# Loading a matrix a second time in turned form, and turning only its solved half on the chip

## The chip, the cores and the metric

The kernel runs on one core of a Trainium2 chip. The metric is the device time of one execution in microseconds (us). A profile of one execution stands beside it: it lists every instruction of the engines TensorE (PE; its weight loads are PEld), VectorE (DVE), ScalarE (ACT), GpSimd (POOL) and SyncE (SP, which here only issues transfers), with the clock that TensorE was granted.

## The reference

Two stages follow one another. The first is a recurrence over 768 time steps, for 4 x 8 heads of width 40:

```
for t in range(S):
    y[:, :, t] = np.einsum('bhd,bhde->bhe', rt, state)
    Sa = np.einsum('bhde,bhe->bhd', state, at)
    state_decay = state * wt[:, :, None, :] - np.einsum('bhd,bhe->bhde', Sa, bt)
    state = state_decay + np.einsum('bhd,bhe->bhde', vt, kt)
```

The second takes the 3072 rows of y (320 wide) as tokens of a mixture of experts: each token goes to the best of 8 experts by x @ w_gate, up to a capacity, through relu(x @ w1) @ w2, scaled by its gate.

## The kernel before

The recurrence is done in chunks of 64 steps: 12 chunks (q), each for two halves of the batch (pr 0 and 1), so 24 units of 16 heads each. Two chunks make one iteration i (128 steps, 6 of them). Per iteration the rows w, a, k and b are loaded and decayed (`decay`, `decay_k`, on DVE), products of the chunk with itself are made (`nn`, `kk`, `iden`), and a triangular system is inverted (`inverse`, `join`, `comb`, mostly a chain on DVE). Per unit a chain then follows, which the state ties to the unit of the chunk before:

1. `zz` and `zz_s` multiply v and the state into a right hand side; `sa` applies the inverse; `take_sa` copies the 64 solved rows beside the 64 loaded rows of v in the tile `vu`. So half of the 128 partitions of `vu` holds v and the other half holds what was solved.
2. `uT` turns `vu` with eight TensorE transposes of 128x128; `take_uT` (ACT, in one unit DVE) copies the result from PSUM to the tile `vT`, 128x1024. There is one `vT`.
3. `mT` multiplies `vT` by `rv`; `take_m` masks it into `vu`; `yy` makes the output rows and the new state; `take_snew` and `take_y` take these.

The output is gated (`gate`, `logits`), routed (`route`: tables of rows for each expert), and stored to `xd`. The experts then gather rows from `xd`, turn them by a transfer, and multiply: `p00` and `p10` are the first parts of experts 0 and 1, whose tokens come from the first four iterations; `p01`, `p11`, `p2` to `p7` follow and need the whole table. Their weights are loaded, and split by ACT and DVE into two halves of 16 bits, in the buffers that the recurrence gives up (`hand_...`).

All engines run in the order of one list, `ORDER`, written out by hand as text. A name is one step, `*2` repeats it, `/1` takes the second choice of engines, and `~3` puts three idle multiplies (`warm`, L197: `ident` by `ident`, 128x512) ahead of it on TensorE. Each engine works through its own instructions in the order of the list and waits where an operand or buffer is not there. All loads and stores of the recurrence are issued by SP in that order too. They are spaced: `dma` lets a transfer start only when the third last one before it has landed (the fifth last for the first twenty).

Of the kernel before, what the change touches and what calls it, by code (L numbers as in the profile page):

```python
# [10 lines left out]
F32 = mybir.dt.float32  # L11
# [8 lines left out]
P = 128  # L20
# [20 lines left out]
out0 iden1 fill chain1 inverse join/1 out0 load_a join join_sw out0 decay0 join iden1 gate0 join decay0 load_rv
turn1 logie0 uT1 load_kb gate0 join load_kb load_v uT1 out1 gate0*2 join logie0 lower_w out1/1 join out1 zz0 decay0
chain0 lower comb out1 comb out1 iden0 decay_k0 chain0 turn0 comb~1 lower decay_k0 turn0/1 gate0 load_a unit comb
turn1~1 decay1 iden0 gate1*2 load_kb comb decay_k1 logie0 turn1 inverse_0 comb load_v gate1 decay1 zz1*2 logie1~3
comb chain0~2 chain0 chain1*2 decay1 logie1 nn0 uT0*2 load_kb nn0/1 nn1~1 logie1 nn1 nn0 out0 nn0 chain1 load_w
decay_k1 nn1~1 out0/1 chain1 uT1 decay0 load_rv nn1 inverse zz0~1 inverse*2 out0 uT1 inverse out0 out1 inverse*2
chain0 logie0 inverse*2 out0 load_w turn0~1 inverse*2 zz1 chain0 gate1 tk_ chain0~1 out1/1 inverse*2 load_v inverse
kk inverse*3 turn0 inverse gate1 chain0 kk out1 uT0 out1 load_a out1 zz1 chain1 iden1 turn1 uT0 inverse out0 chain1
inverse tk_ iden0~1 iden1 kk inverse out0 chain1 iden0 inverse kk out0~1 chain1/1 iden0 zz0 out0 load_a load_v
join_sw join out0 chain0 join chain0 join decay0 iden0 join gate0 load_kb*2 decay0 uT1 decay_k0 gate0 uT1 gate0  # L50
join*2 load_rv logie1 turn1 join lower_w out1 out1/1 comb iden1 load_kb logie0 load_v comb decay_k0 out1 logie0/1
comb iden1 gate0/1 turn0 decay1 out1 lower comb lower/1 nn0 inverse_0 out1 turn0 unit comb~3 zz1~3 nn0 decay1 comb
decay_k1 logie0 zz1 gate0 decay1 turn1 chain0~1 load_kb comb decay_k1 chain1 nn0 chain0 nn1 chain1 uT0 nn0/1 nn1
uT0/1 logie0 nn1 chain1 out0 chain1 nn1/1 out0/1 uT1 load_rv uT1 gate1~2 turn1 inverse out1 inverse*2 out0 out1/1
gate1 inverse load_v inverse gate1 inverse*2 out1 inverse*2 out0 zz0 chain0 load_v inverse logie1 inverse turn0
inverse out0 chain0 out1 inverse out1 inverse zz1 tk_ load_v logie1/1 inverse gate1/1 inverse chain0*2 inverse zz1
kk inverse*2 uT0 chain1 kk inverse uT0 gate1 iden0 turn0 iden0 chain1 logie1 load_w load_a iden1 tk_ out0 inverse
iden1 chain1 load_w chain1 out0/1 join_sw join kk load_a join out0 decay0 out0 kk/1 join*2 iden0~1 out0 iden0 turn1
decay0 join uT1 join load_kb zz0 turn1 gate0 logie1 uT1 out1~2 gate0 decay0 load_v load_kb lower_w logie0 join gate0
out1/1 comb gate0 chain0 logie0/1 chain0 comb out1 lower decay_k0*2 out1 zz1 logie0 out1 iden1*2 lower decay1 comb  # L60
gate1~5 turn0 logie0 load_rv gate0 comb zz1 decay1 gate1 decay1 comb load_kb gate1 chain1 logie1~1 comb*2 turn0/1
chain0*2 load_kb inverse_0 tk_ decay_k1 load_rv turn1 logie1 chain1/1 turn1/1 nn0 nn1 nn0 load_w chain1 decay_k1 kk
chain1 uT0 nn1/1 kk/1 nn0 nn1 unit uT0 out0 nn0 decay0 nn1 out0/1 inverse*2 uT1~1 out0 logie1 inverse out0 inverse*2
zz0 inverse*2 load_v chain0 uT1 inverse out0 inverse gate1/1 chain0 out1 inverse turn0 load_w out1/1 chain0 inverse
chain0 turn0 inverse*2 load_a out1 inverse*2 logie1 inverse out1*2 zz1*2 uT0*2 chain1*2 iden1 out0 load_a iden1
inverse*2 tk_ inverse kk out0 iden0 kk chain1 load_v iden0 out0 inverse*2 chain1/1 zz0 join out0 iden0 join chain0
gate1 out0 uT1~1 chain0 join_sw/1 decay0 join uT1 join load_rv decay0 out1 out1/1 load_kb gate0~1 iden0 turn1
decay_k0 gate0 turn1/1 gate0 join~1 join*2 load_v out1 comb/1 lower out1 nn0 out1 comb load_kb lower gate0 load_v
comb decay_k0 comb inverse_0 gate0 turn1 lower_w/1 iden1 nn0 comb gate1~2 logie1 iden1 decay1 comb*2 chain0~3
load_kb turn1/1 zz1 gate1 decay1 logie1 turn0 gate1 load_kb zz1 chain1 chain0 uT0 nn0~2 chain1 decay1 uT0 gate1  # L70
chain1 out0 decay_k1 chain1 nn1 turn0 nn0/1 out0/1 logie1 unit nn1 hand_z logie1 decay_k1 uT1 kk nn1~2 uT1 tk_ nn1
out0 inverse load_rv out1 hand_px out0 logie0 kk out0 iden1 logie0 out1/1 logie0 inverse zz0 chain0 inverse*2 iden1
# [272 lines left out]
def scan_part(tc, keep, one, psum, w, a, kb, rv, vt, w_gate, wge, xd, lg, ident, up, SX, route, fill):  # L345
# [116 lines left out]
    def prep(pr, i):  # L462
# [57 lines left out]
        def mul_a():  # L520
            engine().tensor_mul(T["a"][0:R], T["a"][0:R], T["px"][0:R, :, 0:P])  # L521
# [1314 lines left out]
```

## Time and profile before

| | |
|---|---|
| median of 3 runs | 569.18 us (567.82 to 573.0) |
| profiled execution | 565.18 us, of which the span from first to last instruction is 563.5 us |
| mean granted clock of TensorE | 0.986 |
| busy: PE, DVE, ACT, POOL | 515.7, 407.6, 304.5, 124.3 us |
| moved by DMA | 81.34 MB |

Busy time is the time in which an engine works at something that the profile counts. An engine can be less than fully busy and still set the pace, if others always wait for it; which one waits for which is read from the list of waits. TensorE's matrix multiplies overlap in the records, so that the time of a step on TensorE is read from the distance of starts.

### The profile page before, as it was taken

What the parts mean: (1) busy time and instruction counts of PE and PEld (TensorE: products, weight loads), DVE (VectorE), ACT (ScalarE), POOL (GpSimd) and SP (SyncE); (2) the same over time, 40 slices, a digit from 0 to 9 for tenths busy, and PEclk for the clock granted to TensorE, in tenths of its full rate; (3) what the DMA queues carried; (4) which work ended last, traced back from release to release, by engine and by line L of the source; (5) the groups of instructions that cost most, each with busy time, mean ns of one, the idle gap of its engine ahead of it and who ended that gap; (6) DMA issues with size and microseconds to landing.
All of it is one profiled execution on the core that took longest, in us unless ns stands there. A gap on an engine that the chain in (4) does not pass through costs nothing.

```text
span 563.5 us, 24790 instructions
## 1 busy us (share of the span) xinstructions
PE 515.7 (92%) x11145; PEld 383.5 (68%) x11145; DVE 407.6 (72%) x671; ACT 304.5 (54%) x572; POOL 124.3 (22%) x173
## 2 busy tenths in 40 slices
PE   0979899999989999999999997997999999999994
PEld 0545688778968887888888885665746465564652
DVE  8999899898979999989799876771536626444140
ACT  4344547867864688559654544542545435553230
POOL 9400010006001100020110023033265042730113
PEclk9999999999999999999999999898999999999998
DMA  8674055543613652445202328658789594992201
GB/s 267 196 208 123 4 137 173 178 125 121 189 57 101 177 179 59 119 154 151 71 24 76 137 88 219 182 159 230 177 255 229 150 265 151 227 196 88 57 24 53
DMA packets 77769, 81.34 MB, mean 144 GB/s; under 512 B 34684, under 2 KB 58366, under 8 KB 77652
## 3 DMA queue, kind: packets, MB, share of 16 engines
q1 hardware_dynamic: 74324, 70.21, 44.8%
q0 software_dynamic: 3328, 9.44, 5.5%
q8 instruction: 89, 1.46, 1.2%
q14 instruction: 28, 0.23, 0.1%
HBM read 63.90 MB, written 10.88 MB: 133 GB/s over the span
## 4 chain that ended last, share of the span: by engine, by line
PE 20%; issue 18%; DVE 6%; DMA 5%; POOL 5%; POOLq 0%; ACT 0%; SPq 0%; DVEq 0%
PE pp L404 8%; PE pp L1644 5%; POOL out_dram L1518 3%; PE p L1512 3%; DMA xT<-a 2%; DMA a<-xd,ri 2%; POOL a L1489 2%; DMA out_dram<-tk,ri 1%; PE pp L904 1%; PE pp L197 1%; DMA px<-in_moe_w_dram 1%; PE p L942 0%; PE pp L578 0%; DVE ns L1451 0%; PE pp L1036 0%
## 5 line engine op out<-in xcount | busy, mean ns | idle before, releaser
L454 POOL TENSOR_SCALAR_AFFINE_SELECT tk<-tk 64x512 f32<-64x512 f32 x28 | 20.6, 737 | 156.6 <-ACT tk L451 112.4
L1518 POOL DMA_INDIRECT out_dram<-tk,ri x26 | 34.1, 1311 | 94.1 <-ACT tk L1679 69.9
L197 PE MATMUL pp<-ident 128*128 128x512 f16 x145 | 40.8, 394 | 9.0 <-ACT pp L422 3.2
L404 PE MATMUL pp<-a,kb 64*64 64x64 f32 x1536 | 30.8, 224 | 11.9 <-DVE a L521 11.1
L404 PEld LDWEIGHTS pp<-a,kb 64*64 64x64 f32 x1536 | 26.3, 136 | 20.6 <-DVE a L521 13.6
L404 PE MATMUL pp<-vu,bk 128*40 128x104 f32 (+1 forms) x768 | 38.7, 252 | 1.7 <-issue 0.8
L1489 POOL DMA_INDIRECT a<-xd,ri x26 | 27.4, 1053 | 42.9 <-DVE gs L1408 26.4
L404 PEld LDWEIGHTS pp<-vu,bk 128*40 128x40 f32 x768 | 33.0, 117 | 4.6 <-issue 1.6
L1644 PE MATMUL pp<-xT,z 128*128 128x448 f16 (+2 forms) x128 | 30.7, 332 | 5.8 <-DMA xT<-a 5.8
L143 ACT COPY vT<-pp 128x1024 f32<-128x1024 f32 x23 | 23.3, 1013 | 21.7 <-PE pp L904 16.7
L1644 PE MATMUL pp<-xT,ns 128*128 128x448 f16 (+2 forms) x192 | 32.4, 307 | 0.4 <-DVE ns L1451 0.4
L586 ACT ACTIVATE bk<-pp,few 128x320 f32<-128x320 f32 x48 | 22.7, 527 | 16.1 <-PE pp L578 15.2
L143 ACT COPY zs<-pp 64x320 f32<-64x320 f32 x44 | 18.5, 420 | 23.2 <-PE pp L404 21.5
L526 DVE TENSOR_TENSOR kb<-kb,gx 104x1024 f32<-104x1024 f32 x24 | 28.9, 1216 | 2.1 <-DMA kb<-in_kb_dram 2.0
L508 DVE TENSOR_TENSOR_SCAN gx<-px,z 104x1032 f32<-104x1032 f32 (+1 forms) x13 | 27.7, 2140 | 1.6 <-DMA px<-in_w_dram 1.2
L147 ACT ACTIVATE ns<-pp 32x256 f32<-32x256 f32 (+1 forms) x51 | 23.0, 450 | 11.0 <-PE pp L404 10.0
L1512 PEld LDWEIGHTS <-px 128*128 128x128 f16 (+1 forms) x256 | 21.4, 100 | 10.8 <-issue 3.4
L404 PE MATMUL pp<-rv,vT 64*64 64x64 f32 x1536 | 28.1, 221 | 0.4 <-ACT vT L143 0.2
L516 DVE TENSOR_TENSOR_SCAN px<-px,z 104x1032 f32<-104x1032 f32 x12 | 27.7, 2307 | 0.4
L458 DVE TENSOR_TENSOR vu<-pp,mask 128x1024 f32<-128x1024 f32 x21 | 25.6, 1217 | 3.0 <-PE pp L404 2.9
L1512 PEld LDWEIGHTS <-nt 128*128 128x128 f16 (+1 forms) x248 | 21.0, 101 | 9.2 <-issue 1.6
L404 PEld LDWEIGHTS pp<-rv,vT 64*64 64x64 f32 x1536 | 24.8, 135 | 3.3 <-issue 0.9
(267 smaller groups left out, 1369.4 us busy)
## 6 DMA issues: line engine op xcount, KB each, us to landing
vu<-in_moe_w_dram SPq DMA_DIRECT2D x32, 320.0 KB, 5.8
kb<-in_kb_dram SPq DMA_DIRECT2D x44, 224.0 KB, 3.3
px<-in_moe_w_dram SPq DMA_DIRECT2D x13, 512.0 KB, 3.7
vu<-in_vt_dram SPq DMA_DIRECT2D x48, 128.0 KB, 3.7
rv<-in_rv_dram SPq DMA_DIRECT2D x24, 256.0 KB, 4.5
xd<-x SPq DMA_DIRECT2D x24, 192.0 KB, 3.5
a<-in_a_dram SPq DMA_DIRECT2D x20, 224.0 KB, 3.3
px<-in_w_dram SPq DMA_DIRECT2D x12, 258.0 KB
```

The source lines that it names most:

```text
L143: (e.copy if e is self.nc.scalar else e.tensor_copy)(out, in_)
L147: (e.mul if e is self.nc.scalar else e.tensor_scalar_mul)(out, in_, x)
L197: self.nc.tensor.matmul(x, self.spare[:, 0:P], self.spare[:, None, :].to_broadcast([P, 2, 2 * P]), start=True, stop=True, skip_group_check ...
L404: TT.matmul(out, l, r, start=start, stop=True, skip_group_check=True)
L458: V.tensor_mul(out, in_, m.to_broadcast(sh))
L508: V.tensor_tensor_scan(T["gx"][0:R, o][:, ::-1], T["px"][0:R].rearrange("p h t -> p (h t)")[:, o][:, ::-1], z2[0:R].rearrange("p h t -> p ...
L516: V.tensor_tensor_scan(T["px"][0:R].rearrange("p h t -> p (h t)"), T["px"][0:R].rearrange("p h t -> p (h t)"), z2[0:R].rearrange("p h t -> ...
L526: engine().tensor_mul(x, x, g[:, :, None, half(c)].to_broadcast([R, H, 2, C]))
L1489: nc.gpsimd.indirect_dma_start(out=xt(j)[:c].rearrange("p a c -> p (a c)"), out_offset=None, in_=src[:, :], in_offset=bass.IndirectOffsetO ...
L1512: nc.tensor.matmul(po[z], h(l, f + z), rr(f + z, 1)[:, 0], start=(f == 0 and m == 0), stop=(f == NF - n and m == 2), skip_group_check=True)
L1518: nc.gpsimd.indirect_dma_start(out=out_v[used[0] % (8 * E)][:, :], out_offset=bass.IndirectOffsetOnAxis(ap=ri.bitcast(U32)[:c, j, 1:2], ax ...
L1644: nc.tensor.matmul(s_["h", f + z][:, :n], l, rr, start=m % 7 == 0 and m < 14, stop=m >= 14)
```

## The change

The host puts a second copy of v in device memory, `vq`, already turned in the way that `uT` would turn it. A new step `load_u` loads one unit of it into a second half `vh` of the tile that held `vT` (also one buffer). `uT` turns only the 64 solved rows, `take_uT` copies only 512 columns, and `mT` takes its left operand from `vh` for the loaded rows and from `vT` for the solved ones. Later stages take the tile over (`hand_vT`) when both halves are free. `mul_a` and `mul_kb` name DVE where they asked the list for it (they ran on DVE before as well). `ORDER` is new as a whole.

```diff
 def uT():
     p = U["pt"] = get("pp")
     for k in range(4):
         for x in range(2):
-            TT.transpose(p[:, x, k * P:k * P + P], U["vu"][:, x, k, C:3 * C], ident)
+            r = half(1 - x ^ pr)
+            TT.transpose(p[:, x, k * C:k * C + C], U["vu"][r, x, k, C:3 * C], ident[r, r])
 def take_uT():
     U["vT"] = get("vT")
-    copy(flat(U["vT"]), U["pt"].rearrange("p x t -> p (x t)"))
+    copy(U["vT"].rearrange("p (x k) t -> p x (k t)", x=2), U["pt"][:, :, 0:4 * C])
...
+        def load_u():
+            x = U["vh"] = get("vh")
+            y = flat(x)
+            if id(x) in whole:
+                for r in (slice(0, D), slice(P - D, P)):
+                    dma(y[r], vq[pr, q, r])
+            else:
+                for o in (slice(0, 256), slice(256, 512)):
+                    dma(y[:, o], vq[pr, q, :, o])
+                whole.add(id(x))
+        steps(f"load_u{pr}")(load_u, "L0>.5&L0>.5", take=["vh"], needs=[("px", (0, 0))] * (q < 2), gives=("load_u", n))
...
 # mT
-                            mm(p[half(z), r, u * C:u * C + C], U["vT"][half(r), u, half(z)], T["rv"][half(r), c, u, :],
-                               True)
+                            y = U["vh" if z == x ^ pr else "vT"]
+                            mm(p[half(z), r, u * C:u * C + C], y[half(r), u], T["rv"][half(r), c, u, :], True)
             put("vT", U["vT"])
+            put("vh", U["vh"])
...
-        more(mT, "P1.5", needs=[("uT", n), ("load_rv", (pr, i))], take=["pp"], free=["vT"])
+        more(mT, "P1.5", needs=[("uT", n), ("load_u", n), ("load_rv", (pr, i))], take=["pp"],
+             free=["vT", "vh"])
...
-            engine().tensor_mul(T["a"][0:R], T["a"][0:R], T["px"][0:R, :, 0:P])
+            V.tensor_mul(T["a"][0:R], T["a"][0:R], T["px"][0:R, :, 0:P])
...
-chain0*2 kk uT0 inverse uT0 kk/1 inverse uT1 out0 inverse*2 uT1 zz0~3 inverse*2 out1 out0/1 out0 inverse*2 out1/1
+nn1~8 nn1 nn0~1 nn0/1 chain1 chain0 chain1/1 nn1 chain0 nn1 chain0/1 load_g uT0~2 inverse*2 load_rv inverse uT0
```

Three places show how the instructions move. The first is SP's queue where the first units need their turned v (`vT<-in_vq_dram` is `load_u`, into `vh`; `vu<-in_vt_dram` is `load_v`; `xd<-x` stores results). Before:

```order
L157 DMA vu_148<-in_vt_dram 64x4x128 x2
L157 DMA vu_150<-in_vt_dram 64x4x128 x2
L157 DMA xd<-tbl 768x1x128 x8
L157 DMA a_124<-in_a_dram 112x512 x2
L157 DMA rv_130<-in_rv_dram 128x512 x2
```

Now:

```order
L159 DMA rv_130<-in_rv_dram 128x512 x2
L159 DMA rv_131<-in_rv_dram 128x512 x2
L159 DMA vT<-in_vq_dram 40x512 x2
L159 DMA vu_151<-in_vt_dram 64x4x128 x2
L159 DMA vu_148<-in_vt_dram 64x4x128 x2
L159 DMA vT<-in_vq_dram 40x512 x2
L159 DMA vu_150<-in_vt_dram 64x4x128 x2
L159 DMA a_124<-in_a_dram 112x512 x2
L159 DMA vT<-in_vq_dram 40x512 x2
```

Each unit has its pair of `vq` transfers between the loads of `vu`, `a` and `kb`, and one pair waits on SP until the `mT` before has freed `vh`; the loads listed behind it wait with it.

The second is TensorE in the last iteration, between the `mT` of pr 1 (the rows with `rv_131,vT`) and the next `mT` of pr 0 (`rv_130,vT`); `yq_142,tm_132` is a table of the routing, `ident,vu` is `uT`. Before:

```order
L404 MATMUL pp_114<-rv_131,vT_153 64x64 x32
L404 MATMUL pp_113<-zs_152,nt_140 64x2x40 x8
L1145 MATMUL p_1_116<-yq_142,tm_132 128x96 x4
L404 MATMUL pp_114<-vu_151,tk_134 64x40 x16
L904 MATMUL pp_112<-ident,vu_150 128x128 x8
L404 MATMUL pp_113<-rv_131,Sd_155 40x64 x16
L404 MATMUL pp_113<-vu_149,bk_144 40x104 x16
L404 MATMUL pp_112<-rv_130,vT_153 64x64 x32
```

Now:

```order
L409 MATMUL pp_114<-rv_131,vT 64x64 x32
L1165 MATMUL p_0_115<-yq_142,tm_132 128x96 x4
L922 MATMUL pp_112<-ident,vu_150 128x64 x8
L409 MATMUL pp_113<-rv_131,Sd_154 40x64 x16
L409 MATMUL pp_113<-vu_149,bk_144 40x104 x16
L409 MATMUL pp_114<-vu_151,tk_134 64x40 x16
L409 MATMUL pp_112<-rv_130,vT 64x64 x32
```

The eight transposes are half as wide, and one product (`zs,nt`) now stands ahead of the first `mT`. (A multiply of 32 bits is one row here and two in the trace.)

The third is DVE at the end of the recurrence, from the table of the fourth iteration (`tbl`, then the index `gs`, `ri` for `p00` and `p10`) to the last `take_y` (the last row with `px_123`, 104x8x64). Before:

```order
L1393 TENSOR_TENSOR tbl<-tbl,p_0_115 128x96
L1403 TENSOR_SCALAR gs_6464<-tbl 128x12
...
L1451 SCALAR_TENSOR_TENSOR kb_129<-vu_148,a_124 128x640
L1451 SCALAR_TENSOR_TENSOR px_119<-px_121,z_167 128x1024
L1393 TENSOR_TENSOR tbl<-tbl,p_1_116 128x96
L143 COPY px_122<-p_0_115 128x128
L994 TENSOR_TENSOR px_123<-pp_113,px_123 104x8x64
L1059 SCALAR_TENSOR_TENSOR x_0_156<-pp_114,x_0_156 128x320 x2
L458 TENSOR_TENSOR vu_151<-pp_112,mask 128x2x8x64
L994 TENSOR_TENSOR px_123<-pp_113,px_123 104x8x64
```

Now:

```order
L1418 TENSOR_TENSOR tbl<-tbl,p_1_116 128x96
L1428 TENSOR_SCALAR gs_6542<-tbl 128x12
...
L145 COPY Sd_154<-p_1_116 128x320
L463 TENSOR_TENSOR vu_151<-pp_113,mask 128x2x8x64
L1418 TENSOR_TENSOR tbl<-tbl,p_0_115 128x96
L1079 SCALAR_TENSOR_TENSOR x_0_155<-pp_112,x_0_155 128x320 x2
L1013 TENSOR_TENSOR px_123<-pp_114,px_123 104x8x64
```

Less of DVE's work stands between the index and the last `take_y`: two splits of weights (L1451) and one of the `take_y` have moved ahead of the index.

## Rows read from the trace of the kernel before

**Rows 1.** Stretch, length, busy us of PE, PEld, DVE, ACT, POOL, clock, DMA.
```profile
66.00:119.50 53.50, 51.39 (x1616) 43.38 (x1613) 49.24 (x68) 37.90 (x72) 2.62 (x4) 1.00 0.53 149
223.50:275.10 51.60, 50.35 (x1664) 43.36 (x1666) 44.33 (x67) 35.78 (x70) 5.25 (x8) 1.00 0.40 122
345.00:351.00 6.00, 2.59 (x56) 2.02 (x56) 1.94 (x4) 0.85 (x1) 1.80 (x2) 0.90 1.06 275
351.00:357.00 6.00, 5.95 (x30) 3.83 (x30) 2.33 (x5) 2.54 (x7) 0.00 (x0) 0.53 0.92 235
410.00:540.00 130.00, 129.35 (x862) 73.27 (x856) 58.80 (x83) 57.61 (x97) 48.02 (x40) 1.00 0.67 171
```
**Rows 2.** Waits of DVE, 25 to 340 us: who for whom, total us, times, longest.
```profile
DVE ns L147 <- PE pp L404: 4.1, 3, 2.6
...
DVE kb L526 <- DMA kb<-in_kb_dram: 2.0, 1, 2.0
...
DVE zs L143 <- PE pp L404: 0.2, 1, 0.2
```
**Rows 3.** Waits of ACT, 60 to 340 us.
```profile
ACT vT L143 <- PE pp L904: 16.2, 12, 4.0
```
**Rows 4.** Groups by line and shape: count, busy us, mean ns of one, idle before.
```profile
L904 PE MATMUL pp<-ident,vu 128*128 128x128 f32 x192 | 25.7, 278 | 0.8 <-DVE tm L1379 0.5 <-DVE px L994 0.3
L143 ACT COPY vT<-pp 128x1024 f32<-128x1024 f32 x23 | 23.3, 1013 | 21.7 <-PE pp L904 16.7 <-issue 2.2 <-DVE yq L1388 1.4
L143 ACT COPY Sd<-p 128x320 f32<-128x320 f32 x16 | 6.9, 431 | 1.0 <-PE p L942 0.9
```
**Rows 5.** Timeline of weight loads and multiplies: start, us, engine, line, shape, count.
```profile
129.32 0.86 PEld L904 LDWEIGHTS pp<-ident,vu 128*128 128x128 f32 x8 [0.15 <-issue]
139.51 0.74 PEld L578 LDWEIGHTS pp<-ident,kb 104*128 104x128 f32 x8 [0.15 <-issue]
509.88 0.65 PE L1644 MATMUL pp<-xT,gx 128*128 128x448 f16 x3
```
**Rows 6.** PE in 40 ns stretches there, L1644 alone: instructions under way (x).
```profile
510.12:510.16 0.04, 0.04 (x1) 1.00 0.00 0
510.16:510.20 0.04, 0.04 (x3) 1.00 0.00 0
```
**Rows 7.** Timeline of PE: idle multiplies, and neighbouring steps mT.
```profile
20.99 1.04 PE L197 MATMUL pp<-ident 128*128 128x512 f16 x4
68.25 1.16 PE L404 MATMUL pp<-rv,vT 64*64 64x64 f32 x64 [0.23 <-ACT vT L143]
70.72 1.14 PE L404 MATMUL pp<-rv,vT 64*64 64x64 f32 x64
326.31 1.16 PE L404 MATMUL pp<-rv,vT 64*64 64x64 f32 x64
333.43 1.16 PE L404 MATMUL pp<-rv,vT 64*64 64x64 f32 x64
127.77 1.63 PE L404 MATMUL pp<-vu,bk 128*40 128x104 f32 x32
338.21 1.13 PE L1145 MATMUL p<-yq,tm 128*128 128x96 f32 x8
```
**Rows 8.** DMA issues: count, KB each, median us to landing; a store's issue on SP.
```profile
vu<-in_vt_dram SPq DMA_DIRECT2D x48, 128.0 KB, 3.7
rv<-in_rv_dram SPq DMA_DIRECT2D x24, 256.0 KB, 4.5
302.47 0.81 SPq L157 DMA_DIRECT2D xd<-x  x2
```
**Rows 9.** Timeline: index of p00, its first multiply, first multiply of p01.
```profile
339.69 0.17 DVE L1403 TENSOR_SCALAR gs<-tbl 128x12 f32<-128x12 f32 x1
351.05 0.61 PE L1644 MATMUL pp<-xT,z 128*128 128x256 f16 x2 [2.58 <-DMA xT<-a]
387.64 0.50 PE L1644 MATMUL pp<-xT,z 128*128 128x192 f16 x2 [3.26 <-DMA xT<-a]
```

More of the change, by code (lines that the diff above doesn't have):

```diff
@@ L41 @@
[L41 to L45, printed above, removed]
@@ L51 @@
[L51 to L55, printed above, removed]
@@ L56 @@
[L56 to L60, printed above, removed]
@@ new lines @@
+inverse kk/1 iden1 inverse*2 load_v kk~2 inverse load_v inverse*4 kk/1 iden1 inverse load_w iden1~12 inverse load_a
+load_kb inverse*2 zz1~1 inverse*2 iden0~4 inverse load_a iden0 inverse*3 iden0~10 load_kb iden0 inverse*3 join_sw
+join iden1 load_kb chain1 join/1 decay0 load_kb join~12 decay_k0*2 join join~9 load_w*2 decay0 join*2 lower_w comb
+lower comb/1 decay1 lower nn0~10 comb~4 comb decay1 inverse_0 zz0~5 decay_k1 nn0 comb~3 decay1 unit comb*2 decay_k1
+nn1~8 nn1 nn0~1 nn0/1 chain1 chain0 chain1/1 nn1 chain0 nn1 chain0/1 load_g uT0~2 inverse*2 load_rv inverse uT0
@@ new lines @@
+inverse join/1 load_w load_v chain0 load_rv chain1 uT1 decay0 turn1/1 chain0 iden0 uT1 join out1~1 join iden0
+gate0~2 load_kb out1/1 load_kb load_u0 join*2 gate0 decay0 gate0 join out1 join comb/1 comb lower/1 out1 gate0/1
+lower_w comb*2 decay_k0 iden1 turn1 lower/1 out1 load_a decay_k0 comb turn1 iden1 decay1*2 comb gate0 logie0~5 nn0
+gate1 load_v comb chain0 logie1 load_kb inverse_0 nn0 load_kb zz1 chain0 zz1 gate1 uT0~1 chain1 decay_k1 uT0 chain1
+logie1 unit gate1 out0 logie1 decay1 decay_k1 tk_ load_v logie1 nn1 load_u1 out0 nn0 nn1/1 logie0 nn0 nn1 nn1/1 kk
@@ L525, in mul_kb @@
             x = T["kb"][0:R, c]
-            engine().tensor_mul(x, x, g[:, :, None, half(c)].to_broadcast([R, H, 2, C]))
+            V.tensor_mul(x, x, g[:, :, None, half(c)].to_broadcast([R, H, 2, C]))
             if c:
@@ L1009, in chain @@
         more(uT, "P.9", needs=[("vu", n)], take=["pp"])
-        more(take_uT, "A1.04|V1.2", take=["vT"], free=["pp"], gives=("uT", n))
+        more(take_uT, "A.56|V.65", take=["vT"], free=["pp"], gives=("uT", n))
         if q:
@@ L1208, in scan_part, with hand_v @@
         hand("rv", "rv", 1, ["hh"], [("load_rv", (pr, last)) for pr in range(2)])
-    for y in ("xt",):
-        hand("vT", "vT", 1, [y], [("uT", (pr, NQ - 1)) for pr in range(2)])
+    def hand_v():
+        get("vT"), get("vh")
+        put("xt", flat(turned_v))
+    steps("hand_vT")(hand_v, "", needs=[(x, (pr, NQ - 1)) for pr in range(2) for x in ("uT", "load_u")],
+                     take=["vT", "vh"], free=["xt"])
     for y in (["sv", "sv"], ["W", "W"], ["W", "W"], ["sv", "W"]):
```

165 lines of the change are left out of this document (89 added, 76 removed).

## Prediction

> **What bounds the kernel now.** I read the busy times by stretch first. In the experts TensorE is busy 129.35 of 130 us [rows 1]; there the kernel is as fast as TensorE, and the change leaves that work alone. What it can move is the time at which the experts begin. So the recurrence counts. From 66 to 303 us (five iterations' worth, of which two stretches stand in the rows) TensorE is busy 51.39 of 53.5 and 50.35 of 51.6 us, VectorE 49.24 and 44.33 [rows 1]: both are close, TensorE closer. The waits say who keeps whom waiting. VectorE's waits between 25 and 340 us on TensorE are ten lines, from 4.1 down to 0.2 us, together 17.0 us, with one wait of 2.0 us on a load [rows 2]. ScalarE waits 16.2 us for the transposes of `uT` alone [rows 3]. So everybody waits for TensorE, while TensorE idles 2.1 and 1.3 us in the two stretches. It also runs idle multiplies of the list, so its queue is not full of needed work; it is the order in which steps come that binds, with TensorE as the engine that is waited for. A microsecond taken from TensorE in the recurrence is therefore worth most of a microsecond, up to the 17.0 us after which VectorE has nothing left to wait for.
>
> The join of the two stages is the other place. The index of `p00` is ready at 339.7 us and its first multiply starts at 351.05, 11.4 us later, through gather and turning transfer [rows 9]. [...] `p01` waits 3.26 us in the same way [rows 9].
>
> **The transposes.** The 24 `uT` are 192 instructions now [rows 4]; eight of them issue over 0.86 us, about 0.103 us apart ((0.86 - 0.14)/7, with 0.14 us for the last load) [rows 5]. Those of `iden` have 104 moving columns beside the same 128 columns of weights and are (0.74 - 0.14)/7 = 0.085 us apart [rows 5]. 0.085/0.103 is 0.83 and 104/128 is 0.81: the moving columns set the distance. The changed `uT` has 64 of them, so 0.05 us and 0.41 us for eight. It also uses only half of the rows of the array, the upper and lower half in turn. The trace has one such pair, two multiplies of 64 rows and 128 columns: both begin within the same 40 ns and stand beside each other [rows 6], in the group of three at 509.88 [rows 5]. If the pairs overlap like that, eight take 0.21 us. So a `uT` falls from 0.86 to between 0.41 and 0.21 us: 0.45 to 0.65 us saved, 10.8 to 15.6 us over 24. I take 0.5 us, so 12 us, near the end that needs no overlap.
>
> [...]
>
> **The copy.** `take_uT` costs ScalarE 1013 ns for 1024 columns, and a copy of 320 columns 431 ns [rows 4]; 0.83 ns per column between them makes 0.59 us for 512. That is 0.42 us each, 10 us of ScalarE in all. ScalarE is busy 37.9 of 53.5 us [rows 1] and mostly waits, so I count nothing for its load. The copy does lie on the chain of a unit (`uT`, copy, `mT`, mask, `yy`, new state), which shortens by about 0.5 + 0.4 us; that helps where the chain binds and is within the 17.0 us above.
>
> **Idle multiplies.** The list has 167 of them instead of 152. Four take 1.04 us [rows 7], so about 0.24 each after the first: 15 more are +3.6 us on TensorE. That the list has more of them where there is less work means that not all of the saving became earlier starts.
>
> **The new load.** It adds 48 transfers on SP, 256 KB for the first unit and 160 KB for the others, 3.9 MB beside 81. The bandwidth is there: the DMA share is 0.53 and 0.40 in the recurrence [rows 1]. The danger is that `vh` is single. A unit's load may be issued only when the `mT` before has read the buffer, and the next `mT` needs it landed. From the start of an `mT` that is about 1.0 us for it (1.16 less the tail) [rows 7], 0.8 us for two issues [rows 8], and 3.7 us to landing, as for the 128 KB loads of `vu` (4.5 for 256 KB) [rows 8]: 5.5 us, and I take 5.6. Against it stands the work of TensorE from one `mT` to the next in the new order. At the place that is shown, it is 1.0 (`mT`), 1.0 (table, 1.13 less its tail), 0.4 (`uT`), 0.5, 1.4 (`vu,bk`, 1.63 less its tail) and 0.5 us: 4.9 us [rows 7]. Done so for all 23 distances, with the time between starts of each kind of multiply, the short ones are 4.2, 4.9, 5.1, 5.3, 5.9, 6.1 and 6.2 us; the others are 7 or more. (Before, the same addition gives 2.3 us where the trace has 2.5, from 68.25 to 70.72, and 5.9 where it has 7.1, from 326.31 to 333.43 [rows 7].) With 5.6 us TensorE stands 1.4 + 0.7 + 0.5 + 0.3 = 2.9 us; some of it would have been idle anyway, so 2.5. Bounds: nothing, if the real distances are as much longer as the last of these; 9 us from start to start, if the spacing of loads adds the landing of another, gives 31 us.
>
> Behind a waiting `load_u` on SP stand loads of `vu`, `a`, `kb` and late in the recurrence of weights. They have slack: VectorE waited for loads of `kb` once, 2.0 us [rows 2], and I count nothing. Without that slack each would cost up to the 3.7 us of a landing.
>
> **The rest of the list.** Adding up VectorE's instructions in the new order with the durations of the old gives 330.9 us to the last `take_y` where it was 330.0: its load does not change. But the index of `p00` stands after 327.1 us of it, against 323.6. So if VectorE led, the experts would begin 3.5 us later. After the last table there are 14 steps of `p10` before `p01`, where there were 12, which covers about 1 us more of the 3.26 us wait [rows 9]; the longer idle before `p00` takes about as much. I count zero for the two.
>
> **Sum.** -12 + 3.6 + 2.5 = -5.9 us, say -6. The profiled execution took 565.2 us (span 563.5), so 559 us in its terms; the median of the runs is 4 us higher at 569.2, so 563 us.
>
> **Rivals.**
> - *The overlap comes in full and the loads hide.* -15.6 + 3.6 and 1 us for `p01`: -13 us, 556. For it: the pair in [rows 6], and distances in the trace that are longer than my sums. Against it: only 17.0 us of VectorE's waits are there to be taken.
> - *VectorE takes over.* It works 49.24 of 53.5 us [rows 1]; if its queue, not TensorE's, sets the time of the index, the 3.5 us more ahead of it eat most of what its shorter waits give: 0 +- 3 us, 569. For it: the idle multiplies, which stand where TensorE is ahead of the others. Against it: its waits [rows 2].
> - *The single `vh` makes the kernel slower.* Each distance is stretched to the turn of the buffer. The place is the first `mT` pair and the pairs of the last three iterations; it pays back the 8.4 us of the first two terms when the turn takes 6.6 us (2.4 + 1.7 + 1.5 + 1.3 + 0.7 + 0.5 + 0.4 = 8.5), and at 7.5 us it costs 15, so 576. For it: 4.5 us landing and the spacing of loads. Against it: 3.7 us for loads of this kind [rows 8].
> - *The narrower transposes cost what the wide ones did*: +3.6 + 2.5 = +6 us, 575. [...] `iden` at 0.085 us speaks against it [rows 5].
>
> **How the numbers follow.** The forecast -6 us (-9 to -3, 560 to 566) has 0.5, the full gain 0.17, VectorE 0.2, the single buffer 0.08, transposes without gain 0.05. A measurement of this kernel can tell about 1% from no change, 5.7 us. A little over half of the forecast's share and the full gain lie beyond that: 0.28 + 0.17 = 0.45 faster. The rest of the forecast and VectorE's case make 0.42 the same, and the last two 0.13 slower. The range goes from 554, the full gain, to 573, past VectorE's case; about 2 in 10 are left out.
>
> **What would show it.** Eight transposes of `uT` that issue over 0.2 to 0.45 us; the copy at 0.59 us; VectorE's waits on TensorE below 17 us; `mT` waiting for a load at no more than some four places, together 2 to 3 us; the first multiply of `p00` 4 to 8 us earlier than 351. The prediction fails if TensorE waits for `vT` loads by more than 8 us, if `uT` still issues over 0.7 us, or if the index of `p00` is no earlier than 339.7 although TensorE works less.

## The result, and the profile after

The changed kernel is slower: 577.07 us median (20 runs, 569.82 to 585.03) against 568.9 of before (20 runs, 563.6 to 577.99); the ratio of the undisturbed runs is 1.012 (95% interval 1.0085 to 1.0155). Ratios below are of that kind, always to the kernel before run beside it, and 0.01 is 5.7 us. The profiled span grew from 563.5 to 572.4 us, the index of `p00` comes at 346.19 us, where it came at 339.69 [rows 9], and the first multiply of `p00` at 359.82, where it came at 351.05.

What was made smaller did become smaller. Timeline of weight loads of one `uT` and of its copy on ScalarE (start, length, engine, line), and the group of all `uT`:

```profile
80.94 0.33 PEld L922 LDWEIGHTS pp<-ident,vu 64*128 64x128 f32 x8
```
```profile
81.45 0.59 ACT L145 COPY vT<-pp 128x512 f32<-128x512 f32 x1 [0.23 <-PE pp L922]
```
```profile
L922 PE MATMUL pp<-ident,vu 64*128 64x64 f32 x192 | 11.5, 235 | 0.4 <-DVE vu L145 0.2
```

Eight transposes issue over 0.33 us instead of 0.86 [rows 5], and the copy takes 0.59 us instead of 1.01 [rows 4]. The stretches (as in [rows 1]: length, busy us of PE, PEld, DVE, ACT, POOL, clock, DMA):

```profile
66.00:119.00 53.00, 49.28 (x1651) 40.64 (x1654) 48.05 (x70) 31.78 (x65) 3.52 (x6) 1.00 0.42 127
224.00:277.00 53.00, 48.38 (x1609) 41.00 (x1610) 47.35 (x73) 31.50 (x63) 3.21 (x6) 0.97 0.42 132
345.00:351.00 6.00, 4.78 (x104) 3.76 (x106) 1.58 (x7) 2.71 (x4) 3.05 (x3) 1.00 0.98 342
351.00:357.00 6.00, 4.75 (x73) 3.47 (x72) 2.67 (x5) 2.01 (x5) 1.22 (x2) 0.68 0.75 157
410.00:540.00 130.00, 126.08 (x873) 73.48 (x871) 61.06 (x91) 59.61 (x105) 43.50 (x36) 1.00 0.69 173
```

TensorE now idles 3.7 and 4.6 us in stretches of the recurrence where it idled 2.1 and 1.3, and 3.9 us in the experts, where it idled 0.65. VectorE's waits on TensorE between 25 and 340 us add up to 20.9 us, where they were 17.0 [rows 2]; the three largest are shown. ScalarE still waits 14.7 us for `uT` (16.2 before [rows 3]):

```profile
DVE ns L149 <- PE pp L409: 5.1, 3, 2.9
DVE D L950 <- PE pp L409: 4.3, 2, 2.4
DVE vu L463 <- PE pp L409: 4.0, 7, 0.8
```
```profile
ACT vT L145 <- PE pp L922: 14.7, 10, 3.5
```

**A line that the prediction did not read** says where the time went: TensorE's waits that end in "issue", that is, on nothing that the profile shows. Between 60 and 340 us, before and after (total, times, longest):

```profile
PE pp L404 <- issue: 5.6, 11, 2.3
```
```profile
PE pp L409 <- issue: 7.3, 12, 1.4
PE p L1165 <- issue: 1.9, 1, 1.9
PE p L409 <- issue: 1.8, 1, 1.8
PE pp L595 <- issue: 0.5, 1, 0.5
```

5.6 us before, 11.5 after. I call these the stops. Some of them cost twice, because the granted clock falls behind them. The stop of 1.76 us that ends at 225.42, and the stretches after it:

```profile
225.42 0.29 PE L409 MATMUL p<-pick,px 128*128 128x16 f32 x2 [1.76 <-issue]
```
```profile
224.00:226.00 2.00, 0.58 (x7) 0.34 (x8) 1.96 (x3) 1.93 (x4) 0.00 (x0) 1.00 0.23 82
226.00:228.00 2.00, 2.00 (x54) 1.85 (x56) 1.72 (x3) 1.21 (x3) 0.00 (x0) 0.72 0.04 8
228.00:230.00 2.00, 2.00 (x30) 1.71 (x30) 0.11 (x1) 0.00 (x0) 0.00 (x0) 0.50 0.00 0
```

The clock goes from 1.00 to 0.50 while TensorE is fully busy and VectorE (0.11 of 2 us) waits for it. It is so behind the two longest stops of the changed kernel (1.76 us, and 1.86 us to 321.16, with 0.50 from 324 to 328), but not behind every long one: after the longest of before, 2.33 us, the clock stays.

```profile
159.40 0.22 PE L404 MATMUL pp<-nt,yq 64*32 64x32 f32 x2 [2.33 <-issue]
```
```profile
160.00:162.00 2.00, 2.00 (x42) 1.30 (x40) 1.45 (x2) 1.77 (x5) 0.00 (x0) 1.00 0.03 8
162.00:164.00 2.00, 2.00 (x92) 1.82 (x94) 0.00 (x0) 1.61 (x4) 0.00 (x0) 1.00 0.00 0
```

Summing (1 - granted clock) x length over stretches of 2 us gives an estimate of what the clock costs: 11.9 us between 20 and 540 us, of which 5.1 lie before 340; before it was 5.1, all of it behind 348 us, where the experts begin.

The account of the index, as TensorE's busy and idle time up to it, before and after:

```profile
0.00:339.69 339.69, 308.79 (x9534) 254.65 (x9535) 304.96 (x480) 210.59 (x398) 50.37 (x107) 1.00 0.43 129
```
```profile
0.00:346.19 346.19, 305.55 (x9558) 249.23 (x9558) 305.85 (x477) 200.24 (x400) 36.83 (x93) 0.99 0.47 141
```

Busy time fell by 3.2 us, although the lower clock stretched it by about 5.1: so TensorE's work shrank by 8.4 us, just the -12 + 3.6 of the prediction. Idle time rose from 30.9 to 40.6: 5.9 by the stops, 3.8 by other waits. -8.4 + 5.1 + 5.9 + 3.8 = 6.4, the 6.5 us by which the index is late.

### The profile page after: what moved, and what is told of

It reads as the page before. It is cut to its first block, busy times and chain, and to the rows that moved or that the text cites. A ratio compares the mean times of both kernels' runs of the same rounds, so it can differ in the third digit from the quotient of the medians.

```text
span 572.4 us, 24872 instructions
## 1 busy us (share of the span) xinstructions
PE 515.2 (90%) x11160; PEld 379.5 (66%) x11160; DVE 406.1 (71%) x665; ACT 292.0 (51%) x572; POOL 113.5 (20%) x159
## 3 DMA queue, kind: packets, MB, share of 16 engines
q8 instruction: 89, 1.46, 1.1%
## 4 chain that ended last, share of the span: by engine, by line
PE 52%; issue 19%; DVE 13%; ACT 7%; POOL 4%; DMA 3%; POOLq 0%; DVEq 0%; ACTq 0%
PE pp L409 25%; PE pp L1669 7%; PE p L1537 7%; PE pp L199 4%; POOL out_dram L1543 2%; PE pp L595 2%; ACT ns L149 2%; DVE vu L463 1%; PE pp L1056 1%; PE p L409 1%; PE p L960 1%; DMA kb<-in_kb_dram 1%; PE pp L922 1%; POOL a L1514 1%; PE p L1165 1%
## 5 line engine op out<-in xcount | busy, mean ns | idle before, releaser
L199 PE MATMUL pp<-ident 128*128 128x512 f16 x156 | 43.8, 395 | 8.9 <-ACT pp L427 3.2
L409 PE MATMUL pp<-vu,bk 128*40 128x104 f32 (+1 forms) x768 | 41.1, 262 | 2.4 <-issue 1.3
L409 PEld LDWEIGHTS pp<-vu,bk 128*40 128x40 f32 x768 | 35.4, 123 | 5.2 <-DVE vu L463 1.9
L149 ACT ACTIVATE ns<-pp 32x256 f32<-32x256 f32 (+1 forms) x57 | 25.6, 450 | 17.7 <-PE pp L409 15.9
L145 POOL COPY x<-x 128x128 f16<-128x128 f16 x14 | 5.6, 399 | 143.9 <-ACT x L149 133.0
L1674 ACT ACTIVATE px<-pp 128x448 f16<-128x448 f32 (+2 forms) x32 | 13.5, 450 | 36.5 <-PE pp L1669 29.0
L1669 PE MATMUL pp<-xT,a 128*128 128x448 f16 (+2 forms) x128 | 28.8, 316 | 3.6 <-issue 2.1
L1674 ACT ACTIVATE nt<-pp 128x448 f16<-128x448 f32 (+2 forms) x32 | 13.8, 452 | 31.7 <-PE pp L1669 30.0
L199 PEld LDWEIGHTS <-ident 128*128 128x128 f16 x167 | 15.0, 101 | 22.6 <-issue 10.2
L1537 PE MATMUL p<-kb,nt 128*128 128x320 f16 (+1 forms) x152 | 28.3, 301 | 1.0 <-DVE nt L1677 1.0
```

Of the source, the lines that this page charges most:

```text
L145: (e.copy if e is self.nc.scalar else e.tensor_copy)(out, in_)
L149: (e.mul if e is self.nc.scalar else e.tensor_scalar_mul)(out, in_, x)
L199: self.nc.tensor.matmul(x, self.spare[:, 0:P], self.spare[:, None, :].to_broadcast([P, 2, 2 * P]), start=True, stop=True, skip_group_check ...
L409: TT.matmul(out, l, r, start=start, stop=True, skip_group_check=True)
L1537: nc.tensor.matmul(po[z], h(l, f + z), rr(f + z, 1)[:, 0], start=(f == 0 and m == 0), stop=(f == NF - n and m == 2), skip_group_check=True)
L1669: nc.tensor.matmul(s_["h", f + z][:, :n], l, rr, start=m % 7 == 0 and m < 14, stop=m >= 14)
```

## Experiments

### Which part of the change

Four kernels take the change apart. Without the load (only the first unit is loaded), in the new list and in the old:

```diff
                 for r in (slice(0, D), slice(P - D, P)):
-                    dma(y[r], vq[pr, q, r])
+                    pass
```

`new_list_only` has the new list with the wide `uT`, copy and `mT` of before and no load. The two kernels with the old list have the change's code and the old ORDER, with each `load_u` put a third of the way from one `mT` to the next.

> The changed kernel with its new list and narrow transposes, but only the first unit's turned v is loaded; the other 46 transfers are left out, so mT multiplies old values in 22 of its 24 places. Theory A (traffic: the extra loads delay something that TensorE needs, its instructions above all; between 20 and 355 us TensorE stood 14.5 us with nothing shown that it waited for, before it was 5.8): these gaps fall back to about 6 us, the index of p00 comes at 338 to 341 instead of 346, the time is 566 to 569 us against 569 of before. Theory B (the new list is slower by itself): gaps and index stay as they are in the changed kernel (14, 346), the time 575 to 578. Theory C (the single vh holds mT up): like A, about 8 us faster than the changed kernel, but the gaps inside steps stay and only mT moves.

> The new list with the work of before: wide uT, wide copy, mT from one tile, no second load. Theory A: the list is not at fault, so about the time of before plus the 3.6 us of the added idle multiplies, 569 to 573 us. Theory B: as slow as the changed kernel or slower, since the narrow transposes are gone too: 577 to 585 us (577 + up to 12 for the transposes that are 0.5 us longer each).

> The whole change but in the list of before: narrow uT, narrow copy, second load for all units, each load's step put a third of the way from the mT before it to the mT that needs it, nothing else moved. Theory A: the traffic is the same as in the changed kernel, so 570 to 577 us, with gaps of more than 10 us. Theory B: the list of before with 0.5 us less per uT: 557 to 565 us. A new wait is possible here: loads of vh that stand before others on the transfer queue can hold these up; it would show as VectorE waiting for kb or a.

> As the run with the list of before, but without the second load save for the first unit (mT multiplies old values in 22 of its 24 places): the gain of the narrow transposes and copies alone. Forecast of the prediction for them: 12 us less, 557 us. If the chain through TensorE was not what set the pace, 565 to 569 us.

| kernel | list | uT | load | ratio (95%) | index, us | stops, 60 to 340 |
|---|---|---|---|---|---|---|
| before | old | wide | no | 1 | 339.69 | 5.6 |
| old_list_no_load | old | narrow | no | 0.997 (0.993 to 1.001) | 337.95 | 8.4 |
| old_list_all | old | narrow | yes | 1.018 (1.013 to 1.023) | 346.53 | 7.0 |
| new_list_only | new | wide | no | 1.018 (1.012 to 1.023) | 352.67 | 10.0 |
| new_list_no_load | new | narrow | no | 1.011 (1.007 to 1.016) | 346.42 | 14.2 |
| changed kernel | new | narrow | yes | 1.012 (1.009 to 1.016) | 346.19 | 11.5 |

In the new list the load costs nothing that can be measured (1.012 against 1.011); in the old list it costs 2%, and VectorE waits 8.7 us for `kb` there, 2.0 before. The longest of these waits (VectorE of old_list_all; on SP this load of `kb` stands behind one of `vh`, a store and one of `a`):

```profile
109.50 1.22 DVE L530 TENSOR_TENSOR kb<-kb,gx 104x1024 f32<-104x1024 f32 x1 [5.40 <-DMA kb<-in_kb_dram]
```

The narrow transposes bring 0.3% in the old list, not to be told from nothing, and about 0.7% in the new (the intervals overlap), not 2%. And the list alone, with the work of before, costs 1.8%. Theory C falls: `mT` has no wait on a load in any of them. A alone falls as well, since the new list is slow without the traffic. Up to the index, the narrow transposes took 9.2 us of busy time from TensorE in the new list, and the index came 6.3 us earlier (new_list_only, then new_list_no_load):

```profile
0.00:352.67 352.67, 313.49 (x9554) 258.02 (x9555) 307.67 (x477) 208.05 (x400) 36.36 (x93) 1.00 0.43 130
```
```profile
0.00:346.42 346.42, 304.29 (x9557) 246.66 (x9558) 305.84 (x477) 200.36 (x400) 36.77 (x93) 1.00 0.45 133
```

Why the narrow transposes bring so little in the old list shows in part at one place of it. With wide `uT` the `mT` at 94.56 us takes 1.13 us, and ahead of it lies a small stop in a step that has nothing to do with it; with narrow `uT` it is (weight loads, then multiplies, of old_list_no_load):

```profile
94.99 0.12 PEld L408 LDWEIGHTS pp<-sw,yq 64*48 64x48 f32 x1 [1.16 <-issue]
```
```profile
95.20 1.64 PE L408 MATMUL pp<-rv,vT 64*64 64x64 f32 x62
```

The same instruction of before stops too, for 0.33 us:

```profile
94.36 0.12 PEld L404 LDWEIGHTS pp<-sw,yq 64*48 64x48 f32 x1 [0.33 <-issue]
```

TensorE came to it earlier and left it no earlier, the stop grew from 0.33 to 1.16 us, and the 62 multiplies behind it took 1.64 us for 1.13. That the clock fell there is an estimate from these two times; over the whole time to the index it is 0.99, for 1.00 before. Up to the index TensorE's busy time fell by 8.4 us (308.79 to 300.44), the index came 1.7 earlier, less than the 3 us by which such stretches differ from one execution to the next (see before_new_experts below):

```profile
0.00:337.95 337.95, 300.44 (x9535) 244.87 (x9536) 303.94 (x481) 201.50 (x398) 49.69 (x107) 0.99 0.43 131
```

TensorE's idle time up to there rose by 6.6 us, from 30.9 to 37.5. By the lists of its waits 2.6 of these are on nothing shown (5.8 to 8.4), 2.6 on VectorE (14.0 to 16.6) and 0.7 on ScalarE (10.1 to 10.8). So the stops took a part of the gain; as much went into waits for VectorE.

### What the stops are

The stops sit inside steps, in the middle of groups of multiplies whose operands are there. Counting instructions between neighbouring ones in the changed kernel (multiplies and weight loads, the counts behind PE and PEld):

```profile
168.19:200.66 32.47, 30.46 (x1022) 26.28 (x1021) 29.50 (x47) 19.73 (x41) 3.72 (x8) 1.00 0.41 125
200.66:205.51 4.85, 3.90 (x127) 3.14 (x128) 4.28 (x5) 3.22 (x5) 0.08 (x1) 1.00 0.57 188
205.51:213.50 7.99, 7.57 (x256) 6.65 (x255) 6.76 (x10) 4.45 (x9) 0.58 (x1) 1.00 0.60 195
```

2043, 255 and 511 instructions: 8, 1 and 2 times 256, less a few that these counts leave out; with TensorE's semaphore instructions, which the trace has as well, the distances are 2048, 256 and 512. It is so between all the stops from 60 to 321 us, in both kernels. The page of before has a DMA queue of instructions (transfers, MB, share):

```profile
q8 instruction: 89, 1.46, 1.2%
```

1.46 MB / 89 is 16.4 KB, and 16.4 KB / 256 is 64 bytes for each instruction. 89 x 256 is 22784, and the page counts 22290 multiplies and weight loads of TensorE. So TensorE's instructions arrive in blocks of 256, one transfer each, and I read a stop as a block that is not there yet. In stretches of 0.25 us between 90 and 240 us the transfers of before stand 3.2 to 6.0 us apart, mostly 0.5 to 1.5 us behind the time at which TensorE enters a block. Nine of the eleven stops of before end 2.3 to 2.5 us after the last of these transfers began (the other two 3.0 and 3.2 us). The longest (2.33 us, to 159.40) goes with the transfer that came late, 6.0 us behind the last:

```profile
q8 instruction: 1, 0.02, 24.6%
```

It is the one at 156.75; the block before had been entered at about 154.6. The transfers are not hidden behind the work: the stops between 60 and 340 us add up to 5.6 us in the kernel before, 11.5 in the changed kernel and 20.6 in after_shift_192 (below).

### Time against instructions, and the idle multiplies

```diff
 # idle_at_uT: in ORDER, four more idle multiplies ahead of every uT
-... uT0 ...
+... uT0~4 ...
 # short_at_uT: in uT
+            for k in range(32):
+                r = half(k % 2)
+                mm(p[r, 0, 0:C], ident[r, r], ident[r, r], True)
```

> The kernel of before with four more idle multiplies (128x512) ahead of each of the 24 uT: about 1.0 us of TensorE each (four take 1.04 us in the trace of before), 25 us in all, but only 8 instructions each (four loads, four multiplies), 192 in all. Theory S (supply: TensorE's long stops, which lie whole multiples of 256 of its instructions apart in the traces of before and of the changed kernel, are the ends of blocks of instructions that have not come yet, and a block takes about 4.0 us): 192 instructions are 0.75 block, +3 us, and what the idle multiplies cost beyond falls into time in which TensorE would have stood: +3 to +15 us. Theory T (TensorE's own time is the bound, as the prediction had it): +20 to +25 us. Theory K (neither, a chain over the other engines): 0 to +10 us.

> The kernel of before with 32 more 64x64 multiplies of 32 bits at the head of each of the 24 uT, whose result the transposes overwrite: the form and number of those of one mT, which take 1.0 to 1.1 us of TensorE, so the same 25 us in all as the run with idle multiplies, but 128 instructions each, 3072 in all, 12 blocks of 256. Theory S: 12 blocks of 4.0 us, +40 to +48 us, and stops that add up to far more than 5.8 us. Theory T: +20 to +25 us, like the idle multiplies. Theory K: 0 to +10 us, like the idle multiplies.

1.040 (1.030 to 1.050) and 1.080 (1.068 to 1.092): +23 and +46 us. That looks like theory S, but it isn't, since the short multiplies took twice what I had taken from `mT`:

```profile
84.02 2.07 PE L404 MATMUL pp<-ident 64*64 64x64 f32 x64
```

24 x 2.07 is 50 us. Both runs cost nearly the TensorE time that they add. The idle multiplies came out in theory T's range (20 to 25 us) and beyond that of S (3 to 15); for the short ones, with 50 us added, the two fall together. So S does not hold as it was put. The pair does show an asymmetry in the old list: 25 us added ahead of `uT` cost 23, while 8 taken away brought 2.

```diff
 # before_no_idle, new_list_no_idle: in all of ORDER; before_idle_early: behind the first zz only
-... inverse iden1~2 load_v kk~7 load_v iden0~3 ...
+... inverse iden1 load_v kk load_v iden0 ...
```

> The kernel of before without its 152 idle multiplies, which take about 0.24 us each, 36 us of TensorE. If they only fill time in which TensorE would wait and keep the granted clock up: stretches at 0.5 of the clock in the recurrence, where before has none up to 348 us, and 575 to 590 us. If they cost more than they bring: 555 to 565 us.

> The new list with the work of before (wide transposes, no second load), without its 167 idle multiplies. The new list was 10 us slower than the old one with this work. If the 15 more idle multiplies and where they stand make that difference, this run equals the old list without idle multiplies within 3 us; if it is the order of the steps, it stays 8 to 13 us slower than that.

Without its 152 idle multiplies the kernel of before takes 1.001 (0.996 to 1.006) of its time: 36 us less on TensorE, 17 us lost to the clock before 340 us, and no difference. The stretches at half the clock came as forecast, the longer time did not. The new list without them has no ratio; its four runs lie at 577.86 to 591.17 us, and nothing is concluded from them.

> The kernel of before with idle multiplies only up to the first unit's zz (about 66 us): 98 of the 152 stay, the 54 later ones, about 12 us of TensorE, are left out. Without any idle multiplies the time was that of before, with 17 us lost to a lower clock in the recurrence, 15 of them ahead of 70 us. If TensorE's time were what the recurrence waits for, this run gains 6 to 12 us (557 to 563). If, as with the narrow transposes, time taken from TensorE only turns into time that it waits: 566 to 570.

1.020 (1.015 to 1.026). Work was only taken away, and the kernel became about 12 us slower, with stops of 16.9 us for 5.6. Neither expectation allows that.

### The order of the last part, and the place of the loads

The first two kernels join two lists at the first `p00`: the steps up to it from one, the remaining steps in the order of the other. The third moves each `load_u` in the old list:

```diff
-load_u k: behind step m[k-1] + (m[k] - m[k-1]) / 3       (m: places of mT in the list)
+load_u k: behind step m[k-1] + (m[k] - m[k-1]) * 3 / 4
```

> The changed kernel, whole, with its new list up to the first p00 and from there on the steps that are left in the order of the old list. Between 400 and 540 us TensorE idles 4.8 to 5.1 us in the three kernels run with the new list, 0.2 to 0.6 in the three with the old one, each time where splits of weights come late (nt, px, tk). Theory L (the order of the splits in the new list costs that): idle there below 1 us and 3 to 5 us faster than the changed kernel, 571 to 574 against 569 of before (ratio 1.004 to 1.008 to before). If the splits come late because the recurrence ended late, nothing changes: 575 to 578 (1.012).

> The kernel of before (wide transposes, no second load, old list) up to its first p00; from there on the steps that are left in the order of the new list. Theory L: TensorE idles 4 to 5 us between 400 and 540 us, the time is 3 to 5 us above before (ratio 1.005 to 1.009). Otherwise 1.000.

> As old_list_all (the whole change in the list of before), which was 1.8% slower than before with waits of VectorE for kb of 8.7 us, but each load of turned v stands three quarters of the way from mT to mT instead of a third, so that the transfer queue need not stand at it. Theory Q (the queue that stands at a load of vh holds the loads of kb and a up): VectorE's waits for kb fall to 2 or 3 us and the time to 565 to 571 (0.995 to 1.003). Theory A (the traffic itself delays): 574 to 578 as before. Risk: mT now waits for its load; then TensorE stands ahead of mT, 2 to 4 us at the close pairs.

- new_then_old_experts: 1.005 (1.001 to 1.008), the number that L forecast, but not by its mechanism: TensorE idles 4.2 us between 400 and 540 us, because a split of `vu` now comes 3.1 us late, and the profiled span is 572.5 us. Inconclusive.
- before_new_experts: 1.002 (0.998 to 1.007). TensorE idles 4.6 us in the experts, as L has it, and in the profile the time from `p00` to the end is 216.5 us for 212.4. The ratio doesn't show these 4 us, and old_list_late, whose experts run in the order of before, idles 4.2 us there as well, 3.2 of them at one late split. So the order of the splits is not shown to be the cause. The index came at 336.35, though the instructions ahead of it are those of before: such stretches differ by 3 us from one execution to the next.
- old_list_late: 1.010 (1.007 to 1.014), for 1.018 (1.013 to 1.023) with the earlier loads. The place of the loads seems to count, but the longest wait for `kb` remains (5.56 us), and Q's 565 to 571 us is missed (575). So Q is not shown, and by what way the load costs time in the old list stays open.

A multiply that waits for a split, in the changed kernel and in old_list_late:

```profile
416.55 0.72 PE L1537 MATMUL p<-kb,nt 128*128 128x320 f16 x4 [0.95 <-DVE nt L1677]
```
```profile
432.63 0.30 PE L1536 MATMUL p<-yb,px 128*128 128x320 f16 x1 [3.21 <-DVE yb L1475]
```

### The place of the block ends

A new list, and idle multiplies put in or left out, also change where in the program the multiples of 256 fall. The next runs change that alone. At the very start, where TensorE waits for its first operands:

```diff
+        for _ in range(32):      # 64 instructions; 64, 96 and 128 in the other runs
+            nc.tensor.matmul(x[0:32, 0:32], self.spare[0:32, 0:32], self.spare[0:32, 0:32], start=True, stop=True,
+                             skip_group_check=True)
         for name, que, new, t, pick in order:
```

> The kernel of before with 32 tiny multiplies (32x32, 64 instructions of TensorE with their loads) at the very start, in the first 20 us, where TensorE waits for its first operands anyway; nothing else changes, neither the list nor any work. Theory P (place of the block ends): TensorE's instructions come in blocks of 256, it stands at the end of a block where the next is not there, and which step such an end falls into decides what it costs; 64 instructions ahead move all ends by 64 against the program. Then the stops lie 64 instructions earlier in the program, still multiples of 256 apart, and the time changes by 1% or more in either direction (563 or less, or 575 or more). Theory O (the order of the steps makes the differences between the kernels): the time of before within 0.4%.

> The same with 64 tiny multiplies, 128 instructions. Theory P: another time again, 1% or more away from before or from the run with 64. Theory O: before within 0.4%.

> The changed kernel with 32 tiny multiplies (64 instructions) at the start. Theory P: the changed kernel's 1.2% over before is to a good part the luck of where its block ends fall; this run differs from it by 1% or more (566 or less, or 581 or more against 569 of before). Theory O: 1.010 to 1.014 to before, as it stood.

> The changed kernel with 64 tiny multiplies (128 instructions) at the start. Theory P: differs by 1% or more from the changed kernel or from the run with 64. Theory O: 1.010 to 1.014 to before.

> The kernel of before with 128 tiny multiplies at the start: 256 instructions, one whole block, so that the block ends fall at the same places of the program as in the kernel before. With 64 it was 1.5% slower, with 128 2.7%. Theory P (place of the block ends): back to the time of before, ratio 0.996 to 1.006, stops of 5 to 8 us between 60 and 340 us at the places of before (an index of p00 at 338 to 342). Theory N (more instructions, or tiny multiplies at the start, cost by their number): 1.04 to 1.055, 592 to 600 us.

> The changed kernel with 96 tiny multiplies, 192 instructions. Theory P: a fourth place of the block ends, anything from 0.995 to 1.03 to before; the runs at 0, 64 and 128 gave 1.012, 1.026, 1.026, and if the place is as good as the one the list was made at or better, the changed kernel can come out at 563 to 572 us. Theory N: 1.03 to 1.045.

| instructions ahead | before: ratio (95%) | index | stops | changed: ratio (95%) | index | stops |
|---|---|---|---|---|---|---|
| 0 | 1 | 339.69 | 5.6 | 1.012 (1.009 to 1.016) | 346.19 | 11.5 |
| 64 | 1.015 (1.010 to 1.020) | 350.73 | 12.2 | 1.026 (1.021 to 1.032) | 352.77 | 14.6 |
| 128 | 1.027 (1.021 to 1.033) | 359.37 | 18.2 | 1.026 (1.022 to 1.031) | 354.94 | 20.2 |
| 192 | not run | | | 1.024 (1.017 to 1.030) | 356.94 | 20.6 |
| 256 | 0.997 (0.993 to 1.002) | 340.52 | 7.8 | not run | | |

64 and 128 tiny instructions make the kernel of before 1.5 and 2.7% slower, and 256 of them, more than either, cost nothing. So it is not their number; it is where the blocks end. Four stops of before, and the same four of the run with 256 (timeline of TensorE; line 404 has become 408):

```profile
126.46 0.93 PE L404 MATMUL pp<-a,kb 64*64 64x64 f32 x49 [0.28 <-issue]
130.83 0.60 PE L404 MATMUL pp<-E,a 64*64 64x40 f32 x25 [0.17 <-issue]
231.91 0.74 PE L404 MATMUL pp<-vu,bk 128*40 128x104 f32 x12 [0.78 <-issue]
286.82 0.19 PE L404 MATMUL pp<-E,a 64*64 64x40 f32 x1 [0.15 <-issue]
```
```profile
126.90 0.93 PE L408 MATMUL pp<-a,kb 64*64 64x64 f32 x49 [0.18 <-issue]
131.55 0.60 PE L408 MATMUL pp<-E,a 64*64 64x40 f32 x25 [0.44 <-issue]
231.85 0.73 PE L408 MATMUL pp<-vu,bk 128*40 128x104 f32 x12 [0.73 <-issue]
286.82 0.19 PE L408 MATMUL pp<-E,a 64*64 64x40 f32 x1 [0.40 <-issue]
```

They break the same groups at the same multiply (49, 25, 12 and 1 left). With 128 they fall elsewhere, into an `mT` for one, for 2.51 us, and the clock falls with it:

```profile
155.99 1.12 PE L408 MATMUL pp<-rv,vT 64*64 64x64 f32 x29 [2.51 <-issue]
```
```profile
154.00:156.00 2.00, 0.01 (x3) 0.01 (x2) 1.00 (x1) 1.95 (x3) 0.00 (x0) 0.75 0.34 98
156.00:158.00 2.00, 2.00 (x35) 1.88 (x35) 0.77 (x1) 1.59 (x2) 0.00 (x0) 0.50 0.63 208
```

Theory P holds and N falls; O is wrong where the list is the same, and may still hold for a part of what separates the two lists. For the run with 128, 12.6 us more of stops and 10.3 us of lower clock before 340 us stand against an index that is 19.7 us late. The hope that another place would make the changed kernel the faster one failed: of its four places the one it came with is the best, as with the kernel before, of three. At the same number of instructions ahead the changed kernel is 1.2% slower than the kernel before at 0, 1.1% at 64 and equal at 128; over these three the means are 1.021 and 1.014. So a part of the 1.2% can be the place, and three places are too few to say how large. No run beat the kernel before by more than its interval.

## Why the prediction was wrong

In the prediction's own terms, each from the ratio of two kernels and so good to some 3 us: the narrow transposes and copies brought 3.7 us in the new list (1.018 to 1.011) and 1.7 in the old (0.997), where -12 stood; the list with its idle multiplies cost 10 us (1.018), where 0 and +3.6 stood; the load cost about 0.5 us (1.011 to 1.012), where +2.5 stood. Two steps failed: the worth of a microsecond of TensorE, and the zero for the list.

- **uT and its copy** (0.86 to between 0.41 and 0.21 us, copy 0.59): right, 0.33 and 0.59. (0.86 has the length of the last load in it, 0.41 and 0.21 do not; with it they are 0.50 and 0.29, so the saving of 0.5 us that was taken lies nearer to pairs that overlap than to the end that needs no overlap.) The eight loads, of 128 columns as before, issue over 0.33 us, (0.33 - 0.14)/7 = 0.03 us apart, in pairs, one on each half, with 0.06 us from pair to pair.
- **The sum of TensorE's work** (-12 + 3.6): right, -8.4 us up to the index.
- **"A microsecond taken from TensorE in the recurrence is worth most of a microsecond"**: this step failed. In the old list, with nothing else changed but the first load, 8.4 us were worth 1.7 at the index and 0.997 (0.993 to 1.001) in the time. VectorE's waits on TensorE were read as time that less work on TensorE gives back. Where TensorE stands at a block's end it does not: at the one that ends at 94.99 us in old_list_no_load TensorE came sooner, and the stop grew from 0.33 to 1.16 us. That is a part of it: of the 6.6 us by which TensorE's idle time rose, 2.6 are waits on nothing shown and 2.6 are waits for VectorE. In the new list 9.2 us were worth 6.3 at the index and 3.7 in the time, so the worth hangs on the list; why it is higher there was not settled.
- **"I count zero" for the rest of the list**: failed by 10 us (new_list_only 1.018). The new list moves the block ends, idles TensorE over 4 us more in the experts, which the prediction held to be untouched (why is open), and puts 15 more idle multiplies. How the 1.8% divide between the place of the ends and the order as such was not settled: that would need this list at several places with the work of before.
- **The new load** (+2.5 us, the single `vh`): small as forecast, 0.1% in the new list, but not by its mechanism, for no `mT` waited. The waits behind a `load_u` on SP, counted as nothing, did not grow in the new list (1.8 us for `kb`, 2.0 before); in the old list the load costs 2%, and the waits for `kb` are 8.7 us.
- **Idle multiplies at 0.24 us each**: the price is not shown to be one. Leaving out all of them changed nothing, leaving out 54 cost 2%. That the 54 did it by moving the block ends (108 instructions) is an estimate, from stops of 16.9 us for 5.6; no run moved the ends of that kernel back.
- **The rivals**: the two that forecast a slower kernel, 576 for the single `vh` and 575 for transposes without gain, come nearest to the 577, but not by their mechanisms, for no `mT` waited and the transposes did shrink. "VectorE takes over" (569) does not hold by its 3.5 us more of work ahead of the index: VectorE's busy time up to it is 304.96 and 305.85 us. That VectorE limits as well is seen where work is taken from TensorE in the old list: TensorE's waits for it up to the index rise from 14.0 us to 16.6 (old_list_no_load) and 28.6 (before_no_idle). Of the signs, VectorE's waits on TensorE did not fall below 17 us (20.9), and the last of the failure signs came true: the index no earlier although TensorE works less.

## What to carry to other kernels

Before a gain on TensorE is priced, read its waits on "issue" and count the instructions between them: here they were multiples of 256, and saving time without saving instructions lengthened a wait (0.33 to 1.16 us). Both kernels here ran fastest with the block ends where their lists had them (of three and of four places), so two versions are compared fairly only at several places; 64 or 128 tiny instructions at the start moved it here, and a whole block of 256 was the control. In the kernel before, 1.5 and 2.7% of the time came from the number of instructions ahead alone.

## What the runs showed of the hardware

TensorE took its instructions in blocks of 256 (16.4 KB, one transfer), and stood up to 2.33 us (before) and 2.51 us (before_shift_128) at block ends, in the middle of a group; in the kernel before, moving the ends by 64 or 128 instructions changed the time by 1.5 and 2.7%, moving them by 256 by nothing (0.997, 0.993 to 1.002). Stops of 1.76 and 2.51 us were followed by stretches at 0.50 of the clock, one of 2.33 us was not. Transposes of 64 rows, alternately on the upper and the lower half of the array, issued 0.03 us apart. And 64x64 multiplies on only two of the four quarters of the array took 2.07 us for 64, where those of `mT`, on all four, took 1.16 (those on two also wrote the same 64 columns each time, so the cause is not shown).
